# Linear attention and an ELU feed-forward layer on one core: the two halves of a quad of heads placed in neighbouring loop slots

## Chip, cores and metric

The kernel runs on one NeuronCore of a Trainium2 chip. The time is the device time of one execution in microseconds (us). The profile comes from one further execution of the same program; TensorE is called PE, VectorE DVE, ScalarE ACT, GpSimd POOL and SyncE SP, as in the profile.

## What is computed

Eight batches of eight heads go through a feature-map attention without softmax over the sequence; its output, heads side by side, is the input of a two-layer network with an ELU between.

```python
# q, k, v: (8, 8, 576, 64); w_phi: (64, 128)
def phi(x):
    proj = x @ w_phi
    proj = proj - max(abs(proj), axis=-1)
    return concatenate([exp(proj), exp(-proj)], axis=-1)
q_p, k_p = phi(q), phi(k)
kv, z = k_p^T @ v, sum(k_p, over the sequence)       # per head
x = (q_p @ kv) / (q_p @ z + 1e-6)
# x as (4608, 512); w_in: (512, 2048); w_out: (2048, 512)
h = x @ w_in
out = where(h > 0, h, exp(min(h, 0)) - 1) @ w_out
```

## The kernel before

**Quads.** A quad is four heads of one batch; there are 16 (`NQ`). Of the 576 positions of a head 512 are its main part, and 64 its tail; the tails of four heads of a quad share one tile. Each quad runs through a list of steps (`attention_steps`, L155):

- `transposes` (L159): PE transposes k and q of the quad, DVE copies them to SBUF (`kT`, `qT`).
- `k_head` five times, four heads and the tails (L212): PE projects (`pk`), DVE takes the maxima of absolute values (`m_k`, L203), ACT writes the two exponentials (`EK`, `EKt`, L216).
- `k_scale` (L221): ACT makes the scale factors `em` from `m_k`, and POOL multiplies v with them (`vs` four times, L230; `vst` twice for the tails, L241).
- `q_head` five times (L218): the maxima of q (`m_q`). `q_features` (L249) and `q_features_tail` (L263): PE computes the transposed features `pq`, ACT writes their exponentials (`Eq`, eight; `Eqt`, two) and `w`.
- `kv` twice (L284): PE sums k features times scaled v (`pkv`, L289 and L300), ACT casts it (`kv`, L308).
- `out_head` four times and `out_tail` (L310, L340): PE forms `pn`, DVE combines two of them into `tot` (L332, L338) or `tott`. `divide` (L365): DVE makes `den` and `rec`, POOL multiplies (`x` four times, L377; `xt`, L383). `x_out` (L390): PE transposes x, DVE copies it to `xT`, the input of the feed-forward part.

**Feed-forward (called MoE in the code).** A chunk is the 512 main rows of one batch; a ninth chunk holds all tails. `mm1` (L433) makes one of 16 slices of the hidden layer: four matmuls of 512 columns into `ph`, exponential on ACT (`e_sb`, L446), minus one on POOL (`u_sb`, L448), minimum and maximum on DVE (`gT`, L451). `mm2` (L455), four per chunk, is 16 matmuls of 512 columns into `po`, a copy on ACT (`o_sb`, L467) and a store by SP.

**Order.** The main loop (L494) issues the steps of quad after quad, each from the first step to the last, and between them the units (`mm1`, `mm2`) of the chunk of the batch before: half of the list beside the first quad of a batch, the rest beside the second. What is left runs after the loop. The compiler's scheduler then sets the order on every engine from the dependencies; each engine takes its instructions strictly in that order. All PSUM tiles of the attention share four buffers (`apsum`), those of `ph` and `po` another four (`mpsum`).

**Loads.** k, q, the tails and the weights are loaded by DMAs that POOL issues, v by DMAs that SP issues. Every eighth DMA of POOL shares a semaphore lane with the one eight earlier and waits for its completion before it is issued. `load_tails` (L100) is called for the first four quads (twelve DMAs) and, after `w_in` and `w_out`, for the other twelve quads (twelve DMAs); all of them stand on POOL ahead of the first `vs`.

Of the kernel before, what the change touches and what calls it, by code (L numbers as in the profile page):

```python
# [12 lines left out]
ACT = mybir.ActivationFunctionType  # L13
# [8 lines left out]
def kernel(  # L22
# [53 lines left out]
    w_in_sb = consts.tile([P, N_CT, DFF], BF16)  # L76
    w_in_r = moe_w_in.rearrange("(ct p) j -> p ct j", p=P)
# [21 lines left out]

    def load_tails(g0, g1):  # L100
        for src, dst, eng in (
            (k, k_tails, nc.gpsimd),
            (q, q_tails, nc.gpsimd),
            (v, v_tails, nc.gpsimd),
        ):
            flat = src.rearrange("b (g h) s d -> (b g) h s d", g=2)
            for s in range(2):
                for c in range(2):
                    eng.dma_start(
                        out=dst[s * TAIL:(s + 1) * TAIL, g0:g1, c, 0:D],  # L110
                        in_=flat[g0:g1, 2 * s + c, MAIN:S, :].rearrange(
                            "g j d -> j g d"
                        ),
                    )

# [39 lines left out]
    def attention_steps(i):  # L155
# [92 lines left out]

        def q_features(par, s):  # L249
            pq = apsum.tile([P, 4 * P], FP32, name="pq", tag="ap")  # L250
            nc.tensor.matmul(  # L251
                pq,
                w_phi_both[:, par, :],
                st["qT"][:, 4 * s:4 * s + 4, :].rearrange("p a b -> p (a b)"),
                start=True,
                stop=True,
            )
            for sg in range(2):
                nc.scalar.activation(  # L259
                    st["Eq"][:, par, s, sg, :], pq, ACT.Exp, scale=1.0 - 2.0 * sg  # L260
                )
# [22 lines left out]
        def kv(c):  # L284
# [12 lines left out]
            for s in range(2):  # L297
                for sg in range(2):
                    for t in range(NT):
                        nc.tensor.matmul(  # L300
                            pkv[:, s, sg, :],
                            st["EK"][:, 2 * s + c, sg, t * F:(t + 1) * F],
                            st["vs"][:, 2 * s + c, sg, t, :],
                            start=False,
                            stop=(t == NT - 1),
                            skip_group_check=True,
                        )
            nc.scalar.copy(st["kv"][:, c], pkv)  # L308

        def out_head(hh):  # L310
            s, c = divmod(hh, 2)
            if hh == 0:
# [5 lines left out]
            for sg in range(2):  # L318
                pt = apsum.tile([P, NT, D1], FP32, name=f"pn{sg}", tag="ap")
                for t in range(NT):  # L320
                    tp, par = divmod(t, 2)
                    o = (2 * c + tp) * P
                    nc.tensor.matmul(  # L323
                        pt[:, t, :],
                        st["Eq"][:, par, s, sg, o:o + P],
                        st["kv"][:, c, s, sg, :],
                        start=True,
                        stop=True,
                    )
                pn.append(pt)  # L330
# [34 lines left out]
        def divide():  # L365
# [9 lines left out]
            for hh in range(4):  # L375
                s, c = divmod(hh, 2)
                nc.gpsimd.tensor_tensor(  # L377
# [40 lines left out]
        return (
            [transposes]
            + [each(k_head, hh) for hh in range(5)]  # L420
            + [k_scale]
            + [each(q_head, hh) for hh in range(5)]
            + [each(q_features, par, s) for s in range(2) for par in range(2)]
            + [q_features_tail]
            + [each(kv, c) for c in range(2)]
            + [each(out_head, hh) for hh in range(4)]
            + [out_tail, divide, x_out]
        )

# [48 lines left out]

    def moe_units(ch):
        return [lambda jt=jt: mm1(ch, jt) for jt in range(N_JT)] + [  # L480
            lambda tt=tt: mm2(ch, tt) for tt in range(CHUNK // P)
        ]


    load_quad(0)
    load_tails(0, 4)
    load_quad(1)
    load_w_in()
    load_quad(2)
    load_w_out()  # L490
    load_tails(4, NQ)

    pending = []
    for i in range(NQ):  # L494
# [47 lines left out]
```

## Time and profile before

| | |
|---|---|
| runs (median of 3; lowest, highest) | 574.58 us (571.85, 575.05) |
| the profiled execution: its time, its span | 574.21 us, 572.4 us |
| mean granted clock of PE (1 is 2.4 GHz) | 0.901 |
| busy: PE, DVE, ACT, POOL | 416.2, 292.0, 264.8, 263.3 us |

The span runs from the first to the last instruction; the time of the execution is 1.81 us longer. Busy time is what an engine executes; an engine that waits for a semaphore is idle. The chain of waits follows the last instruction back to what released each step. In the windows the columns after the length are the busy times of PE, of PE's weight loads, of DVE, ACT and POOL with counts, then the granted clock, the share of the DMA engines and GB/s.

### The profile page before, as it was taken

Reading aid. Unit: us, or ns where it says so; the run is one execution under the profiler, and the core shown is the slowest. Engines: PE = TensorE matmul, PEld = TensorE weight load, DVE = VectorE, ACT = ScalarE, POOL = GpSimd, SP = SyncE. Lnnn points to the kernel's source line nnn. Section 1 sums busy time; section 2 is a strip of 40 time slices with the busy share of each in tenths; the row PEclk is TensorE's granted clock in tenths of the full one; section 3 lists DMA queues with packets and bytes.
Section 4 is the critical chain, followed back from the end, with each engine's and each line's share of the span. In section 5 each row is a group of like instructions: output and inputs, shape, how many; then the busy total and the mean of one; then the engine's idle time right before and its main releaser. Section 6 shows DMA issues by size and latency. Waiting matters only on the chain.

```text
span 572.4 us, 8389 instructions
## 1 busy us (share of the span) xinstructions
PE 416.2 (73%) x3066; PEld 232.1 (41%) x3120; DVE 292.0 (51%) x647; ACT 264.8 (46%) x581; POOL 263.3 (46%) x392
## 2 busy tenths in 40 slices
PE   2302557768866786868787896778768867789996
PEld 1102334434443443434344444444435434444443
DVE  2300646484548435763576466836484538527070
ACT  1600244654374518371836265635655373725251
POOL 7637234654365426551556236633644265426060
PEclk9855767799989799999988998999799979899999
DMA  9999312122312215041403231323100100010103
GB/s 161 194 198 137 47 38 37 38 38 73 74 38 38 50 54 82 1 74 57 84 10 57 73 57 38 42 70 74 38 0 35 42 1 2 19 56 1 74 1 73
DMA packets 71496, 32.55 MB, mean 57 GB/s; under 512 B 47904, under 2 KB 66336, under 8 KB 71456
## 3 DMA queue, kind: packets, MB, share of 16 engines
q0 software_dynamic: 32416, 14.19, 21.7%
q1 hardware_dynamic: 39040, 17.83, 11.8%
q8 instruction: 24, 0.39, 0.3%
q14 instruction: 16, 0.13, 0.1%
HBM read 36.77 MB, written 9.44 MB: 81 GB/s over the span
## 4 chain that ended last, share of the span: by engine, by line
PE 31%; POOL 26%; issue 16%; DVE 11%; ACT 9%; DMA 6%; POOLq 0%; ACTq 0%; DVEq 0%
POOL vs L230 11%; PE po L459 11%; PE ph L438 10%; POOL x L377 6%; ACT EK L216 6%; DVE gT L451 4%; POOL vst L241 3%; DMA w_out_sb<-in_moe_w_out_dram 3%; PE tr L167 3%; POOL u_sb L448 3%; DVE tot L332 2%; DVE tot L338 2%; PE pkv L300 2%; PE pk L196 2%; DMA w_in_sb<-in_moe_w_in_dram 2%
## 5 line engine op out<-in xcount | busy, mean ns | idle before, releaser
L438 PE MATMUL ph<-xT,w_in_sb 128*128 128x512 bf16 x482 | 136.1, 394 | 18.0 <-DVE gT L451 16.1
L448 POOL TENSOR_SCALAR u_sb<-e_sb 128x512 bf16<-128x512 f32 x144 | 88.1, 619 | 116.9 <-ACT e_sb L446 105.7
L451 DVE SCALAR_TENSOR_TENSOR gT<-u_sb,ph 128x512 bf16<-128x512 bf16 x144 | 95.7, 681 | 86.5 <-POOL u_sb L448 85.7
L459 PE MATMUL po<-w_out_sb,gT 128*128 128x512 bf16 x554 | 138.9, 389 | 0.8
L446 ACT ACTIVATE e_sb<-ph 128x512 f32<-128x512 f32 x144 | 89.6, 636 | 102.6 <-PE ph L438 79.1
L438 PEld LDWEIGHTS <-w_in_sb 128*128 128x128 bf16 x576 | 55.6, 101 | 68.2 <-issue 31.0
L230 POOL TENSOR_TENSOR vs<-v_main,em 128x520 bf16<-128x520 f32 x64 | 65.7, 1056 | 36.3 <-ACT em L224 36.3
L377 POOL TENSOR_TENSOR x<-tot,rec 128x256 bf16<-128x256 f32 x64 | 37.2, 614 | 92.1 <-DVE rec L374 91.0
L459 PEld LDWEIGHTS <-gT 128*128 128x128 bf16 x576 | 55.4, 100 | 57.9 <-issue 4.2
L216 ACT ACTIVATE EK<-pk 128x512 bf16<-128x512 f32 x128 | 64.6, 633 | 24.3 <-DVE m_k L203 24.3
L467 ACT COPY o_sb<-po 128x512 f32<-128x512 f32 x36 | 21.1, 586 | 114.4 <-PE po L459 114.4
L332 DVE TENSOR_TENSOR tot<-pn,w 128x260 f32<-128x260 f32 x64 | 24.9, 424 | 93.1 <-PE pn L323 92.8
L259 ACT ACTIVATE Eq<-pq 128x512 bf16<-128x512 f32 x128 | 67.6, 712 | 4.7 <-PE pq L251 4.7
L289 PE MATMUL pkv<-vst,EKt 128*128 128x130 bf16 x64 | 11.2, 271 | 72.8 <-POOL vst L241 52.7
L203 DVE TENSOR_REDUCE m_q<-pk 128x4 f32<-128x512 f32 (+1 forms) x80 | 48.4, 634 | 10.0 <-PE pk L196 9.0
L203 DVE TENSOR_REDUCE m_k<-pk 128x4 f32<-128x512 f32 (+1 forms) x80 | 46.4, 630 | 2.8 <-PE pk L196 2.5
L289 PEld LDWEIGHTS <-EKt 128*128 128x128 bf16 x64 | 6.7, 108 | 80.1 <-issue 69.6
L308 ACT CAST kv<-pkv 128x260 bf16<-128x260 f32 x32 | 12.0, 376 | 57.1 <-PE pkv L300 57.1
L196 PE MATMUL pk<-w_phi_both,qT 128*128 128x256 bf16 x144 | 28.1, 301 | 13.0 <-ACT EK L216 11.3
L394 PE MATMUL tr<-ident,x 128*128 128x128 bf16 x128 | 13.5, 232 | 24.9 <-POOL x L377 24.9
L401 DVE COPY xT<-tr 128x1024 bf16<-128x1024 bf16 x16 | 11.1, 692 | 39.2 <-PE tr L394 39.2
L196 PE MATMUL pk<-w_phi_both,kT 128*128 128x256 bf16 x144 | 25.0, 287 | 7.4 <-ACT EK L216 6.5
(61 smaller groups left out, 473.0 us busy)
## 6 DMA issues: line engine op xcount, KB each, us to landing
v_main<-in_v_dram SPq DMA_DIRECT2D x64, 128.0 KB, 2.6
out_dram<-o_sb SPq DMA_DIRECT2D x32, 256.0 KB, 2.3
k_main<-in_k_dram POOLq DMA_DIRECT2D x16, 256.0 KB, 4.4
q_main<-in_q_dram POOLq DMA_DIRECT2D x16, 256.0 KB, 4.9
w_in_sb<-in_moe_w_in_dram POOLq DMA_DIRECT2D x4, 512.0 KB, 9.6
w_out_sb<-in_moe_w_out_dram POOLq DMA_DIRECT2D x4, 512.0 KB, 17.3
out_dram<-o_sb SPq DMA_DIRECT2D x8, 128.0 KB, 2.3
k_tails<-in_k_dram POOLq DMA_DIRECT2D x4, 96.0 KB, 13.8
```

The costliest lines, as they stand in the source:

```text
L196: nc.tensor.matmul(pk[:, 2 * j:2 * j + 2, :].rearrange("p a b -> p (a b)"), xT[:, 2 * hh + j, :], w_phi_rhs, start=True, stop=True,)
L203: nc.vector.tensor_reduce(m[:, 4 * hh:4 * hh + 2 * n], pk[:, 0:2 * n, :], axis=AX.X, op=ALU.max, apply_absolute_value=True,)
L216: nc.scalar.activation(dst, pk, ACT.Exp, scale=1.0 - 2.0 * sg)
L230: nc.gpsimd.tensor_tensor(vs[:, hh], vb[:, hh:hh + 1].to_broadcast((P, 2, NT, D1)), em[:, :, 4 * hh:4 * hh + 4, None].to_broadcast((P, 2, ...
L259: nc.scalar.activation(st["Eq"][:, par, s, sg, :], pq, ACT.Exp, scale=1.0 - 2.0 * sg)
L332: nc.vector.tensor_tensor(tot, pn[1], st["w"][:, 4 * hh:4 * hh + 4, None].to_broadcast((P, NT, D1)), op=ALU.mult,)
L377: nc.gpsimd.tensor_tensor(st["x"][:, s, :, c, :], st["tot"][:, hh, :, 0:D], rec[:, 4 * hh:4 * hh + 4, None].to_broadcast((P, NT, D)), op=A ...
L438: nc.tensor.matmul(ph, w_in_sb[:, ct, jt * P:(jt + 1) * P], xTs[ch][:, ct, :], start=(ct == 0), stop=(ct == N_CT - 1),)
L446: nc.scalar.activation(e_sb, ph, ACT.Exp)
L448: nc.gpsimd.tensor_scalar(u_sb, e_sb, -1.0, 1.0, op0=ALU.add, op1=ALU.mult)
L451: nc.vector.scalar_tensor_tensor(gTs[ch][:, jt, :], u_sb, 0.0, ph, op0=ALU.min, op1=ALU.max)
L459: nc.tensor.matmul(po, gT[:, jt, tt * P:(tt + 1) * P], w_out_sb[:, jt, :], start=(jt == 0), stop=(jt == N_JT - 1),)
```

## The change

The loop now has 17 slots (n = 0 to 16). Slot n issues the first half of quad n (`k_head`, `k_scale`, `q_head`, `q_features`) beside the second half of quad n-1 (`kv`, `out_head`, `out_tail`, `divide`, `x_out`), alternating step by step, and at its end the transposes of quad n+1. The units of a chunk are listed in another way: after every fourth `mm1` of a chunk follows one `mm2` of the chunk before; the last chunk's `mm2` come at the end. The units of the chunk of batch b stand in slots 2b+3 and 2b+4, where they stood beside quads 2b+2 and 2b+3, and each chunk's `mm2` a whole chunk later, so more is left after the loop: 320 matmuls of 512 columns against 256.

The heads of a quad are paired in another way (first and second head instead of first and third in one group), which needs the rows of `w_in` in another order: eight DMAs of 64 partitions instead of four of 128. The tails are loaded by six DMAs per batch, 48 in all against 24. `w_out` is loaded in slot 1 instead of before the loop.

```diff
-            nc.gpsimd.dma_start(out=w_in_sb[:, ct, :], in_=w_in_r[:, ct, :])
+            for c in range(2):
+                nc.gpsimd.dma_start(
+                    out=w_in_sb[c * D:(c + 1) * D, ct, :],
+                    in_=w_in_r[ct // 2, c, ct % 2],
+                )
...
-    def load_tails(g0, g1):
...
+    def load_tails(b):
+        for src, dst in ((k, k_tails), (q, q_tails), (v, v_tails)):
+            heads = src[b].rearrange("(gc s) j d -> s j gc d", s=2)
             for s in range(2):
...
+                nc.gpsimd.dma_start(
+                    out=dst[s * TAIL:(s + 1) * TAIL, 2 * b:2 * b + 2, :, 0:D].rearrange(
+                        "p g c d -> p (g c) d"
+                    ),
+                    in_=heads[s, MAIN:S],
+                )
...
+    def slot_steps(n):
+        new = attention_steps(n) if n < NQ else None
+        old = quads.get(n - 1)
...
+        k = new["k"] if new else [None] * 5
+        qs = new["q"] if new else [None] * 5
+        if old:
+            steps += [old["kv"][0], k[0], old["kv"][1], k[1]]
+            for hh in range(3):
+                steps += [old["out"][hh], k[2 + hh]]
+            steps += [old["out"][3], new and new["scale"][0], old["out"][4]]
+        else:
+            steps += k + new["scale"]
+        steps += qs
+        if old:
+            steps += old["x"]
+        if new:
+            steps += new["qf"]
+            quads[n] = new
+        if n + 1 < NQ:
+            steps.append(lambda: transpose_next(n + 1))
+        return [f for f in steps if f]
...
+    def mixed_units(ch):
+
+        units = []
+        for jt in range(N_JT):
+            units.append(lambda jt=jt: mm1(ch, jt))
+            if ch > 0 and jt % 4 == 3:
+                units.append(lambda tt=jt // 4: mm2(ch - 1, tt))
+        return units
 
     load_quad(0)
-    load_tails(0, 4)
+    load_tails(0)
     load_quad(1)
     load_w_in()
     load_quad(2)
-    load_w_out()
-    load_tails(4, NQ)
-
+
+    transpose_next(0)
     pending = []
-    for i in range(NQ):
...
+    for n in range(NQ + 1):
+        steps = slot_steps(n)
+        share = len(pending) // 2 if n % 2 == 1 else len(pending)
         done = 0
...
+        if n == 1:
+            load_w_out()
+        if n + 3 < NQ:
+            load_quad(n + 3)
+        if n % 2 == 0 and n // 2 + 1 < B:
+            load_tails(n // 2 + 1)
+        if n > 0 and n % 2 == 0:
+            pending.extend(mixed_units(n // 2 - 1))
+    for unit in pending + mixed_units(B):
         unit()
+    for tt in range(CHUNK // P):
+        mm2(B, tt)
```

What the scheduler made of it stands below at three places; a count "x8" means that the instruction follows itself.

POOL at the start, from the load of `w_in` to the first `vs`. Before:

```order
L83 DMA w_in_sb<-in_moe_w_in_dram 128x2048 x4
L137 DMA k_main<-in_k_dram 128x4x256
L137 DMA q_main<-in_q_dram 128x4x256
L87 DMA w_out_sb<-in_moe_w_out_dram 128x4x512 x4
L109 DMA k_tails<-in_k_dram 64x12x64 x4
L109 DMA q_tails<-in_q_dram 64x12x64 x4
L109 DMA v_tails<-in_v_dram 64x12x64 x4
L230 TENSOR_TENSOR vs<-v_main_98,em 128x520 x4
```

Of the change, on to the first `x`:

```order
L84 DMA w_in_sb<-in_moe_w_in_dram 64x2048 x8
L136 DMA k_main<-in_k_dram 128x4x256
L136 DMA q_main<-in_q_dram 128x4x256
L229 TENSOR_TENSOR vs<-v_main_98,em 128x520 x4
L240 TENSOR_TENSOR vst_104<-v_tails,em 64x4x65 x2
L136 DMA k_main<-in_k_dram 128x4x256
L136 DMA q_main<-in_q_dram 128x4x256
L108 DMA k_tails<-in_k_dram 64x4x64 x2
L108 DMA q_tails<-in_q_dram 64x4x64 x2
L108 DMA v_tails<-in_v_dram 64x4x64 x2
L91 DMA w_out_sb<-in_moe_w_out_dram 128x4x512 x3
L229 TENSOR_TENSOR vs<-v_main_100,em 128x520 x4
```

The `vs` of quad 0 moved ahead of `w_out` and of all tails but those of batch 0; eleven DMAs now stand between it and the `vs` of quad 1. The tail loads of the later batches do not follow the batches: behind the first `xt` the scheduler put 23 DMAs in a row (k and q of two quads and 19 of tails) ahead of the `vs` of quad 2, and all the others before the `vs` of quad 3.

POOL in the middle of the program, from one `vs` to the next. Before:

```order
L230 TENSOR_TENSOR vs<-v_main_100,em 128x520 x4
L241 TENSOR_TENSOR vst_104<-v_tails,em 64x4x65 x2
L448 TENSOR_SCALAR u_sb<-e_sb 128x512 x10
L377 TENSOR_TENSOR x<-tot,rec 128x4x64 x4
L383 TENSOR_TENSOR xt<-tott,rec 128x128
L448 TENSOR_SCALAR u_sb<-e_sb 128x512 x2
L137 DMA k_main<-in_k_dram 128x4x256
L137 DMA q_main<-in_q_dram 128x4x256
L448 TENSOR_SCALAR u_sb<-e_sb 128x512
L230 TENSOR_TENSOR vs<-v_main_102,em 128x520 x4
```

Of the change:

```order
L229 TENSOR_TENSOR vs<-v_main_100,em 128x520 x4
L240 TENSOR_TENSOR vst_106<-v_tails,em 64x4x65 x2
L448 TENSOR_SCALAR u_sb<-e_sb 128x512
L376 TENSOR_TENSOR x<-tot,rec 128x4x64 x4
L382 TENSOR_TENSOR xt<-tott,rec 128x128
L448 TENSOR_SCALAR u_sb<-e_sb 128x512 x2
L136 DMA k_main<-in_k_dram 128x4x256
L136 DMA q_main<-in_q_dram 128x4x256
L448 TENSOR_SCALAR u_sb<-e_sb 128x512 x5
L229 TENSOR_TENSOR vs<-v_main_102,em 128x520 x4
```

Before, a `vs` and the `x` behind it belong to the same quad; now that `x` belongs to the quad before, and stands right behind the `vs` of the next one. Every quad has eight `u_sb` beside it; before it was thirteen or three by turns.

ACT in the middle of the program, from one `em` to the next `EK`. Before:

```order
L224 ACTIVATE em<-m_k 128x18 x2
L446 ACTIVATE e_sb<-ph 128x512
L259 ACTIVATE Eq<-pq 128x512 x8
L274 ACTIVATE Eqt<-pq 128x256 x2
L281 ACTIVATE w<-m_q 128x18
L308 CAST kv<-pkv 128x260 x2
L467 COPY o_sb<-po 128x512 x4
L446 ACTIVATE e_sb<-ph 128x512
L216 ACTIVATE EK<-pk 128x512 x8
```

Of the change, on to the next `em`:

```order
L258 ACTIVATE Eq<-pq 128x512 x8
L446 ACTIVATE e_sb<-ph 128x512
L273 ACTIVATE Eqt<-pq 128x256 x2
L467 COPY o_sb<-po 128x512
L307 CAST kv<-pkv 128x260 x2
L215 ACTIVATE EK<-pk 128x512 x2
L446 ACTIVATE e_sb<-ph 128x512
L215 ACTIVATE EK<-pk 128x512 x2
L446 ACTIVATE e_sb<-ph 128x512 x2
L215 ACTIVATE EK<-pk 128x512 x2
L215 ACTIVATE EKt<-pk 128x256 x2
L223 ACTIVATE em<-m_k 128x18 x2
```

The casts of `kv` belong to quad n-1 and stand behind the `Eq` of the same quad, as before; behind them now come the `EK` of quad n, no longer in one run of eight but with `e_sb` between them.

## Rows read from the trace of the kernel before

**Rows 1.** The page, section 1: busy us (share of the span) xinstructions.

```profile
PE 416.2 (73%) x3066; PEld 232.1 (41%) x3120; DVE 292.0 (51%) x647; ACT 264.8 (46%) x581; POOL 263.3 (46%) x392
```

**Rows 2.** Windows of the start, one batch in the middle, and the end; columns as above.

```profile
25.00:52.00 27.00, 0.00 (x0) 0.00 (x0) 0.00 (x0) 0.00 (x0) 14.28 (x18) 0.50 1.84 175
310.07:369.22 59.15, 46.95 (x374) 26.59 (x380) 35.16 (x79) 31.32 (x71) 28.72 (x42) 0.96 0.27 54
540.37:568.00 27.63, 27.47 (x125) 12.32 (x126) 10.92 (x16) 11.89 (x20) 9.88 (x16) 1.00 0.15 39
568.00:572.40 4.40, 0.01 (x1) 0.00 (x0) 0.00 (x0) 0.59 (x1) 0.00 (x0) 0.88 0.25 60
```

**Rows 3.** The chain that ended last, POOL's vs: start, us, what.

```profile
310.07 4.10 POOL vs L230 x4
...
340.98 4.07 POOL vs L230 x4
...
490.62 4.10 POOL vs L230 x4
```

**Rows 4.** Timeline of the start: start, us, engine, what, count [idle before <-releaser].

```profile
4.42 2.47 POOL L109 DMA_DIRECT2D k_tails<-in_k_dram  x4
...
18.91 0.34 ACT L224 ACTIVATE em<-m_k 128x18 f32<-128x18 f32 x2
...
22.62 0.75 POOL L87 DMA_DIRECT2D w_out_sb<-in_moe_w_out_dram  x1 [1.55 <-DMA w_in_sb<-in_moe_w_in_dram]
...
32.73 0.75 POOL L109 DMA_DIRECT2D k_tails<-in_k_dram  x1 [0.65 <-DMA q_main<-in_q_dram]
...
47.44 4.11 POOL L230 TENSOR_TENSOR vs<-v_main,em 128x520 bf16<-128x520 f32 x4
51.51 1.32 POOL L241 TENSOR_TENSOR vst<-v_tails,em 64x260 bf16<-64x260 bf16 x2
...
52.88 0.38 PE L289 MATMUL pkv<-vst,EKt 128*128 128x130 bf16 x2 [31.32 <-POOL vst L241]
...
54.17 0.38 ACT L308 CAST kv<-pkv 128x260 bf16<-128x260 f32 x1 [29.45 <-PE pkv L300]
...
60.70 2.32 POOL L377 TENSOR_TENSOR x<-tot,rec 128x256 bf16<-128x256 f32 x4 [6.35 <-DVE rec L374]
...
62.99 0.39 POOL L383 TENSOR_TENSOR xt<-tott,rec 128x128 bf16<-128x128 f32 x1
```

**Rows 5.** Timeline of one quad in the middle.

```profile
309.04 0.76 ACT L216 ACTIVATE EKt<-pk 128x256 bf16<-128x256 f32 x2
309.57 0.42 ACT L224 ACTIVATE em<-m_k 128x18 f32<-128x18 f32 x2
...
311.50 4.03 ACT L259 ACTIVATE Eq<-pq 128x512 bf16<-128x512 f32 x8 [1.03 <-PE pq L251]
...
315.34 0.74 ACT L274 ACTIVATE Eqt<-pq 128x256 bf16<-128x256 f32 x2
...
315.61 0.68 PE L300 MATMUL pkv<-vs,EK 128*128 128x65 bf16 x16
...
318.57 0.77 DVE L332 TENSOR_TENSOR tot<-pn,w 128x260 f32<-128x260 f32 x2 [1.70 <-PE pn L323]
```

**Rows 6.** Groups of instructions by form: busy us, mean ns | idle before.

```profile
L451 DVE SCALAR_TENSOR_TENSOR gT<-u_sb,ph 128x512 bf16<-128x512 bf16 x144 | 95.7, 681 | 86.5 <-POOL u_sb L448 85.7
L446 ACT ACTIVATE e_sb<-ph 128x512 f32<-128x512 f32 x144 | 89.6, 636 | 102.6 <-PE ph L438 79.1 <-PE pk L196 20.5 <-PE pn L323 2.3
L448 POOL TENSOR_SCALAR u_sb<-e_sb 128x512 bf16<-128x512 f32 x144 | 88.1, 619 | 116.9 <-ACT e_sb L446 105.7 <-DVE tot L338 6.9 <-DVE tot L332 2.3
```

**Rows 7.** PE's timeline behind an idle time in the middle.

```profile
346.38 0.38 PE L289 MATMUL pkv<-vst,EKt 128*128 128x130 bf16 x2 [3.27 <-ACT e_sb L446]
346.55 1.08 PE L300 MATMUL pkv<-vs,EK 128*128 128x65 bf16 x16
```

**Rows 8.** The window on these matmuls; columns as in rows 2.

```profile
346.50:348.00 1.50, 1.32 (x19) 1.13 (x18) 0.93 (x2) 0.83 (x4) 1.50 (x3) 0.50 0.36 82
```

More of the change, by code (lines that the diff above doesn't have):

```diff
@@ L259, in q_features @@
                 nc.scalar.activation(
-                    st["Eq"][:, par, s, sg, :], pq, ACT.Exp, scale=1.0 - 2.0 * sg
+                    st["Eq"][:, par, c, sg, :], pq, ACT.Exp, scale=1.0 - 2.0 * sg
                 )
@@ L301, in kv @@
                             pkv[:, s, sg, :],
-                            st["EK"][:, 2 * s + c, sg, t * F:(t + 1) * F],
-                            st["vs"][:, 2 * s + c, sg, t, :],
+                            st["EK"][:, 2 * c + s, sg, t * F:(t + 1) * F],
+                            st["vs"][:, 2 * c + s, sg, t, :],
                             start=False,
@@ L310, in out_head @@
         def out_head(hh):
-            s, c = divmod(hh, 2)
+            c, s = divmod(hh, 2)
             if hh == 0:
@@ L321, in out_head @@
                     tp, par = divmod(t, 2)
-                    o = (2 * c + tp) * P
+                    o = (2 * s + tp) * P
                     nc.tensor.matmul(
                         pt[:, t, :],
-                        st["Eq"][:, par, s, sg, o:o + P],
+                        st["Eq"][:, par, c, sg, o:o + P],
                         st["kv"][:, c, s, sg, :],
@@ L375, in divide @@
             for hh in range(4):
-                s, c = divmod(hh, 2)
+                c, s = divmod(hh, 2)
                 nc.gpsimd.tensor_tensor(
@@ L416, in each @@
             return lambda: f(*a)
[L418 to L428, printed above, removed]
+        return {
+            "tr": [transposes],
+            "k": [each(k_head, hh) for hh in range(5)],
+            "scale": [k_scale],
+            "q": [each(q_head, hh) for hh in range(5)],
+            "qf": [each(q_features, par, c) for c in range(2) for par in range(2)]
+            + [q_features_tail],
+            "kv": [each(kv, c) for c in range(2)],
+            "out": [each(out_head, hh) for hh in range(4)]
+            + [lambda: (out_tail(), divide())],
+            "x": [x_out],
+        }
     gTs = {}
@@ L477, in mm2, with transpose_next, attention_steps @@
                 )
[L479 to L482, printed above, removed]
+    def slot_steps(n):
+        new = attention_steps(n) if n < NQ else None
+        old = quads.get(n - 1)
+        nxt = []
+        steps = []
+        k = new["k"] if new else [None] * 5
[16 more added lines that the diff above has]
+        return [f for f in steps if f]
+    quads = {}
+    ready = {}
+    def transpose_next(n):
+        ready[n] = build_steps(n)
+        ready[n]["tr"][0]()
+    build_steps = attention_steps
+    def attention_steps(n):
+        return ready.pop(n)
+    def mixed_units(ch):
[5 more added lines that the diff above has]
+        return units
     load_quad(0)
-    load_tails(0, 4)
+    load_tails(0)
     load_quad(1)
@@ L489 @@
     load_quad(2)
-    load_w_out()
-    load_tails(4, NQ)
+    transpose_next(0)
     pending = []
-    for i in range(NQ):
-        b, qd = divmod(i, 2)
-        steps = attention_steps(i)
-        share = len(pending) if qd == 1 else len(pending) // 2
+    for n in range(NQ + 1):
+        steps = slot_steps(n)
+        share = len(pending) // 2 if n % 2 == 1 else len(pending)
         done = 0
-        for n, step in enumerate(steps):
+        for j, step in enumerate(steps):
             step()
-            upto = share * (n + 1) // len(steps)
+            upto = share * (j + 1) // len(steps)
             while done < upto:
```

25 lines of the change are left out of this document (3 added, 22 removed).

## The prediction

> **What bounds the kernel now.** I read the engine totals first: PE is busy 73% of the span, no other engine above 51% [rows 1]. None is full, so the time is made of waits, and the question is where. The windows by stage tell that [rows 2]. In 25 to 52 us PE executes nothing at all. In the middle a batch (two quads and one chunk) takes 59.15 us, in which PE is busy 46.95, DVE 35.16, ACT 31.32 and POOL 28.72 us. In the last windows 128 matmuls of 512 columns take 27.63 us with PE busy 27.47: there PE is the bound, at 0.216 us per matmul and a clock of 1.00. The chain of waits names what the middle waits for: a `vs` on POOL leads every quad, at 310.07, 340.98 and, six quads after the first of these, at 490.62 [rows 3], so a quad takes 180.55 / 6 = 30.1 us. The timeline of the start names the first wait: POOL issues `w_out` and the later tails before the first `vs`, waiting for landings, until 47.44; PE has waited 31.32 us for `vst` when it goes on at 52.88 [rows 4].
>
> **The change, 1: the start.** The first `vs` now stands behind k and q of quad 2, not behind `w_out`. The q load waits for the second half-load of `w_in`, which is the first quarter of `w_in` together with the one before it; that quarter had landed at 22.62 [rows 4]. Six tail DMAs fewer stand ahead, for which I take off 2 us, and one issue (0.75) follows: `vs` at 21.3. Its `em` was ready at 19.3 [rows 4]. `vs` and `vst` take 4.11 and 1.32, so the first `kv` matmul moves from 52.88 to about 26.8, the cast behind it, at 54.17, to 28. Four more `w_in` issues are covered by the same waits for landings; without the cover they would be some 2 us.
>
> **2: slots 1 to 4.** I count a slot from the first `kv` cast to the next one. In slot 1 POOL issues eleven DMAs before the `vs` of quad 1, the third `w_out` only when the first new tail has landed. Quad 2's q had landed at 32.73 with twelve tails ahead [rows 4], now some 30.7; behind it k and q of quad 3 and the tail, 1.3 us each: `vs` at about 35.5, done 40.9, one more issue, `x` and `xt` (2.32 and 0.39 [rows 4]) done 44.4. Then comes what I call the return: transposes, first `pq`, eight `Eq` in 4.03, two `Eqt` in 0.74 [rows 5], cast: 6 us without MoE work. Slot 2 begins at 51. There POOL first issues 23 DMAs, four at 0.75 and 19 at 2.47 / 4 = 0.62 [rows 4], 14.8 us: `vs` of quad 2 runs from 59.2 to 64.6, a tail DMA and `x` to 68, the return to 75. Issued in slots 4, 6 and on, as the text of the loop reads, these loads would cost the same issues later; here they hold one `vs` by 2 us at most, as its `em` is ready at 57. Slots 3 and 4 have eight `mm1` and no `mm2` each: I take 25 us, between this slot and the full one below. Slot 5 begins at 125.
>
> **3: a full slot.** Eight `mm1` and two `mm2` beside one quad. The time is not a sum of an engine's work but a ring through the fixed orders of ACT, DVE and POOL, which comes back to the `kv` cast:
> - From the first cast to the last `m_k`: the second `kv` group and its cast end 1.0 later. ACT then does two `EK`, 1.0 (eight `Eq` in 4.03 give 0.5 for each that follows another [rows 5]), and an `e_sb` of 0.64; `u_sb` takes 0.62 [rows 6]; the `gT` for it stands on DVE ahead of the third `m_k`. From there DVE has in a row: three `gT` and two `m_k` of 0.6 (0.68 for a `gT` alone, less the overlap [rows 6]), four `tot` operations of 0.4 [rows 5], a short `m_k` of 0.4, with one `gT` more already under way: 5.0. Sum 8.2.
> - `EKt` and `em`: 0.76 and 0.42 [rows 5] with the hand-over, 1.3.
> - POOL: `vs`, `vst` 5.4, one `u_sb` 0.6, and only then `x`, `xt` 2.7 [rows 4]: 8.7. `rec`, which `x` needs too, is ready some 2 us before POOL comes to it, so POOL's order is what ends last.
> - The return, with an `e_sb` and an `o_sb` in ACT's order and the `mm2` matmuls on PE that wait for the PSUM buffers of `Eq`: 0.7 + 4.0 + 0.5 + 0.75 + 1.1 + 0.4 = 7.5, with hand-overs 7.7.
>
> Together 26 us against 30.1: the pipelining takes the long `vs` wait out of the quad's own chain, but `x` of the quad before now queues behind it. PE's own work is less: 64 matmuls at 0.216 are 13.8; the attention of a quad is at most (46.95 - 27.6) / 2 = 9.7 [rows 2], and by its 15,568 columns at the rate of the last window 6.6. So PE has 20.4 to 23.5 us of work in 26 and is not the bound. Slots 5 to 15: 11 x 26 = 286. Slot 16 begins at 411.
>
> **4: the end.** Behind the last first cast PE has half a chunk's list (64 matmuls) and the 320 left after the loop: 384 x 0.216 = 82.9, and some 2.7 for the last quad's second half. The last copy and store stay at 4.40 [rows 2]. Sum: 411 + 82.9 + 2.7 + 4.4 = 501, and 1.8 us around the span: 503. The profiled execution took 574.21, the median is 574.58: the sum stands on nearly the same time. I take **502 us**.
>
> The new order of `w_in`'s rows and of the heads costs nothing in the steps: the instructions keep their forms and counts. The other price the trace does not show is that of more semaphore hand-overs in the ring: zero if all hide, 0.1 for each of twenty if none does: 24 to 28 us per slot, 480 to 524 in all.
>
> **The rivals.**
> (a) *PE becomes the bound.* If DVE and ACT run ahead of the orders I followed, a slot lasts as long as PE's work, 20.4 to 23.5, say 22. Then 11 x 4 us come off: 458. For it: PE has the most work in every window of the middle. Against it: `x` cannot start before `vs` ends on POOL. The Trainium skill, Perfetto Trace Analysis, Optimization Strategy, says that interleaving stages with different limiting engines may improve the time; in the trace the middle and the end do have different limits [rows 2], but the ring is a limit of no engine's total.
> (b) *The wait before `x` cools PE.* In each slot PE runs out of matmuls some 2 to 3 us before `x` is ready. After an idle time of 3.27 us, 16 `pkv` matmuls ran with a granted clock of 0.50, which is 1.2 GHz, and took 1.08 us instead of the 0.68 in the quad shown [rows 5, 7, 8]. In the return PE has about 5 us of work at full clock; if it mostly runs at half, the slot grows by 3 us: 502 + 33 = 535. Against it: in the middle the clock was 0.96 on the mean, with such waits in it [rows 2].
> (c) *The lower clock holds through the slot.* Then the kernel gets slower: with a share f of PE's 22 us at half clock a slot takes 22 (1 + f). The old time is reached when eleven slots take 72 us more, that is 32.5 us, f = 0.48; at f = 0.6, with 35 us, it is 601. For it: the units, once in runs, are cut into ones and twos between small matmuls of the attention. The Trainium skill, Perfetto Trace Analysis, Matmul Optimizations, says that the matmul engine scales its power with use and that matmuls should come in back-to-back batches; by that rule this rival's side gains. Against it: the window of one batch has the same small matmuls and 0.96.
> (d) *The change does not do what it says.* For the tail loads that is so (they are not spread over the batches), and counted above. For the halves the orders on ACT and POOL show the new interleaving; I give it no chance of its own.
>
> **How the numbers follow.** Forecast (24 to 28 us a slot) 0.62; (a) 0.16; (b) 0.18; (c) 0.04. Range 457 to 536: it holds the forecast's case, most of (b) and the upper half of (a). A difference of 0.5% is about what a measurement of this kernel can tell from none (its three runs spread by 0.56%). Only (c) ends on the slow side: faster 0.96, same 0.01, slower 0.03.
>
> **What would show it.** Right: `vs` starts at about 21 us and every 26 us in the middle; `x` follows `vst` and one `u_sb` on POOL without a gap; the window of a batch lasts 52 us; after the last `x` some 73 us of dense PE. Wrong: `x` waiting for `rec` rather than for POOL (my DVE part is too short), a granted clock near 0.5 behind each `x` wait (b, c), PE without idle time in the middle (a), or a first `vs` well behind 21 us.

## The result and the profile after

The changed kernel takes **508.8 us** (median of 4 runs, 507.1 to 509.8) against 573.2 for the kernel before on the same chip: ratio **0.888, 95% interval 0.883 to 0.893**. That is 64 us or 11.2% faster. Predicted were 502 us, range 457 to 536. The profiled execution took 507.1 us, with a span of 505.3. The page, section 1 and the clock by slices, which answer to [rows 1]:

```profile
span 505.3 us, 8410 instructions
PE 409.6 (81%) x3070; PEld 223.1 (44%) x3120; DVE 306.1 (61%) x647; ACT 268.3 (53%) x581; POOL 278.5 (55%) x420
PEclk9965959797989899989999999999998999899999
```

PE has nearly the same matmuls and the same busy time as before, in a span 67 us shorter. Windows of the changed kernel, which answer to [rows 2] (start, one batch in the middle, the end and what follows it; columns: start:end, length, then busy us and count of PE, PEld, DVE, ACT, POOL, the granted clock, DMA share, GB/s):

```profile
27.00:52.00 25.00, 14.44 (x113) 8.73 (x112) 11.42 (x28) 9.91 (x23) 19.42 (x29) 0.59 1.30 189
229.00:280.00 51.00, 45.47 (x367) 25.16 (x372) 36.38 (x78) 31.43 (x70) 28.79 (x42) 0.97 0.33 63
411.00:430.00 19.00, 16.53 (x125) 8.49 (x126) 11.18 (x25) 6.50 (x13) 7.63 (x13) 0.99 0.07 28
430.00:500.00 70.00, 69.69 (x313) 31.47 (x318) 21.92 (x32) 25.99 (x44) 19.77 (x32) 0.98 0.14 45
500.00:505.30 5.30, 0.54 (x3) 0.04 (x1) 0.00 (x0) 0.59 (x1) 0.00 (x0) 0.94 0.24 56
```

The start, where PE did nothing, now holds 14.44 us of its work. A batch (two slots, 24.9 and 26.5) takes 51.4 us instead of 59.15, with nearly the same busy times. The kernel leaves 64 matmuls more for the end; at the 0.216 us each of the dense stretch [rows 2] they are 13.8 us (an estimate) by which the end is longer.

Where the time went is read off three points: the first `kv` cast, the same cast of the last quad, and the end. Before, the first cast stood at 54.17 [rows 4], and the last quad's was this row of ACT's timeline:

```profile
496.88 0.38 ACT L308 CAST kv<-pkv 128x260 bf16<-128x260 f32 x1 [0.20 <-PE pkv L300]
```

After, the two rows are:

```profile
27.69 0.38 ACT L307 CAST kv<-pkv 128x260 bf16<-128x260 f32 x1 [4.83 <-PE pkv L299]
...
411.14 0.51 ACT L307 CAST kv<-pkv 128x260 bf16<-128x260 f32 x1
```

So the start gave 54.17 - 27.69 = 26.5 us. The fifteen quads between took 442.7 us before and 383.4 now (29.5 and 25.6 each): 59.3 us. The end took 75.5 us before and 94.2 now: 18.7 us given back. Together 67.1 us, the difference of the two spans (572.4 and 505.3).

### The profile page after: what moved, and what is told of

Same layout as the page of the kernel before. It is cut to its first block, busy times and chain, and to the rows that moved or that the text cites. A ratio compares the mean times of both kernels' runs of the same rounds, so it can differ in the third digit from the quotient of the medians.

```text
span 505.3 us, 8410 instructions
## 1 busy us (share of the span) xinstructions
PE 409.6 (81%) x3070; PEld 223.1 (44%) x3120; DVE 306.1 (61%) x647; ACT 268.3 (53%) x581; POOL 278.5 (55%) x420
## 4 chain that ended last, share of the span: by engine, by line
PE 52%; POOL 20%; DVE 13%; DMA 6%; issue 4%; ACT 4%; POOLq 0%; ACTq 0%
PE po L459 22%; PE ph L438 13%; POOL x L376 7%; DMA q_main<-in_q_dram 5%; POOL vs L229 4%; DVE m_q L202 4%; PE pq L250 4%; PE pn L322 3%; PE pkv L299 2%; POOL vst L240 2%; PE pk L195 2%; ACT EK L215 2%; POOL u_sb L448 2%; PE tr L166 2%; DVE den L367 2%
## 5 line engine op out<-in xcount | busy, mean ns | idle before, releaser
L459 PE MATMUL po<-w_out_sb,gT 128*128 128x512 bf16 x559 | 148.1, 389 | 1.8 <-DVE gT L451 1.4
L438 PE MATMUL ph<-xT,w_in_sb 128*128 128x512 bf16 x480 | 131.0, 390 | 4.6 <-DVE gT L451 3.4
L446 ACT ACTIVATE e_sb<-ph 128x512 f32<-128x512 f32 x144 | 87.3, 611 | 48.8 <-PE ph L438 46.8
L215 ACT ACTIVATE EK<-pk 128x512 bf16<-128x512 f32 x128 | 69.4, 612 | 13.1 <-DVE m_k L202 13.0
L202 DVE TENSOR_REDUCE m_k<-pk 128x4 f32<-128x512 f32 (+1 forms) x80 | 50.4, 632 | 25.9 <-PE pk L195 25.6
L322 PEld LDWEIGHTS <-Eq 128*128 128x128 bf16 x512 | 28.9, 98 | 24.9 <-issue 17.0
L393 PEld LDWEIGHTS <-x 128*128 128x128 bf16 x128 | 8.4, 108 | 68.8 <-POOL x L376 68.8
L322 PE MATMUL pn<-kv,Eq 128*128 128x65 bf16 x512 | 34.0, 194 | 3.8 <-ACT EK L215 2.6
L136 POOL DMA_DIRECT2D k_main<-in_k_dram x16 | 12.8, 802 | 35.9 <-PE tr L166 25.3
L195 PE MATMUL pk<-w_phi_both,kT 128*128 128x256 bf16 x144 | 29.6, 284 | 3.3 <-ACT EK L215 1.0
L171 DVE COPY kT<-tr 128x1024 bf16<-128x1024 bf16 x16 | 11.1, 692 | 34.1 <-PE tr L166 34.1
```

The source lines that it names most:

```text
L195: nc.tensor.matmul(pk[:, 2 * j:2 * j + 2, :].rearrange("p a b -> p (a b)"), xT[:, 2 * hh + j, :], w_phi_rhs, start=True, stop=True,)
L202: nc.vector.tensor_reduce(m[:, 4 * hh:4 * hh + 2 * n], pk[:, 0:2 * n, :], axis=AX.X, op=ALU.max, apply_absolute_value=True,)
L215: nc.scalar.activation(dst, pk, ACT.Exp, scale=1.0 - 2.0 * sg)
L322: nc.tensor.matmul(pt[:, t, :], st["Eq"][:, par, c, sg, o:o + P], st["kv"][:, c, s, sg, :], start=True, stop=True,)
L438: nc.tensor.matmul(ph, w_in_sb[:, ct, jt * P:(jt + 1) * P], xTs[ch][:, ct, :], start=(ct == 0), stop=(ct == N_CT - 1),)
L446: nc.scalar.activation(e_sb, ph, ACT.Exp)
```

## The experiments

Eleven kernels were run, each against the kernel before on the same chip, in several runs of each. The ratios can therefore be compared across the groups. "Against the change" below is the ratio less 0.8879, times 573.2 us; the intervals of a ratio are 0.003 to 0.007 either way, so a difference below some 4 us is not told from none.

| run | median us | ratio (95%) | against the change, us |
|---|---|---|---|
| the change | 508.8 | 0.888 (0.883 to 0.893) | |
| e1_no_pipeline | 558.0 | 0.976 (0.972 to 0.980) | +50 |
| e2_unmixed | 515.4 | 0.902 (0.899 to 0.905) | +8 |
| e3_w_out_early | 520.4 | 0.911 (0.906 to 0.916) | +13 |
| e4_pool_before_x | 517.3 | 0.905 (0.901 to 0.909) | +10 |
| e5_pool_after_x | 508.1 | 0.888 (0.882 to 0.894) | 0 |
| e6_x_before_vs | 513.0 | 0.897 (0.892 to 0.903) | +5 |
| e7_q_heads_late | 532.9 | 0.932 (0.926 to 0.937) | +25 |
| e8_both | 490.9 | 0.859 (0.852 to 0.866) | -17 |
| e9_busy_wait | 523.5 | 0.918 (0.914 to 0.921) | +17 |
| e10_tails_held | 500.7 | 0.878 (0.875 to 0.882) | -6 |
| e11_both_held | 485.2 | 0.851 (0.847 to 0.855) | -21 |

### The parts of the change, undone one by one

**The pipelining** (the loop over quads runs all steps of a quad in sequence again; the new loads and the mixed units stay):

```diff
-    for n in range(NQ + 1):
-        steps = slot_steps(n)
...
+    for n in range(NQ):
+        b, qd = divmod(n, 2)
+        st = build_steps(n)
+        steps = [
+            f
+            for part in ("tr", "k", "scale", "q", "qf", "kv", "out", "x")
+            for f in st[part]
+        ]
```

> The steps of a quad stand one after another again; the mixed list of units, the new loads and the pairing of heads stay. Theory (the ring through ACT, DVE and POOL; the start and the pipelining are two separate gains): the start keeps its gain of 26 us, a quad takes its own chain of about 30 us again, so 545 to 555 us. Rival (the mixed units and the new loads bring the gain, the two halves side by side little): at most 520 us.

Measured 558.0 us, a ratio of 0.976: 3 us beyond what was expected, and far from the rival. By the same three points (casts at 28.03 and 467.99, span 555.7) the start keeps its 26 us and a quad takes 29.3 us, as before (29.5), so the theory held there; what it left out is the end, 87.7 us against 75.5. So the early start and the mixing alone leave 2.4% of the 11.2%; some 50 of the 64 us hang on this edit. It is not the pipelining alone: the transposes are no longer made a slot ahead, and `w_out` is loaded in slot 0. The first `vs` starts as early as in the change, at 21.30, but the second only at 55.82 (38.44 in the change). Its `em` had been ready since 46.8; POOL's load issues, three of them waiting 1.9 to 2.2 us each for `w_out`, held it 9 us. Behind this first slot a slot takes 29.0 us on the mean of fourteen, against 25.5 in the change: 48 us, the price of the pipelining together with the early transposes.

**The mixing** (all `mm2` of a chunk behind its `mm1` again):

```diff
-            if ch > 0 and jt % 4 == 3:
-                units.append(lambda tt=jt // 4: mm2(ch - 1, tt))
+        for tt in range(CHUNK // P):
+            units.append(lambda tt=tt: mm2(ch, tt))
```

> The two halves stay side by side; the units of a chunk are listed as before, 16 mm1 and then 4 mm2, so that a slot has ten mm1, or six mm1 and four mm2, by turns. Theory: a slot follows the ring, in which an e_sb more or less moves POOL's and DVE's part by some 0.6 us each, up and down by turns, and 64 matmuls fewer are left after the loop: 500 to 514 us. Rival (the mixing is what lets PE run on, without it the mm1 slots are bound by DVE): 530 us or more.

Measured 515.4 us: the rival falls, and the theory's range is missed by 1 us on the slow side. The mixing is worth 8 us on balance. From the casts (27.97 and 433.78) and the span (513.6), a slot without it takes 27.1 us on the mean instead of 25.6, which is 22 us over fifteen slots, and the end, with 64 matmuls fewer, is 14 us shorter (79.8 against 94.2). That longer and shorter slots would balance was wrong.

**The late `w_out`** (loaded ahead of the loop again):

```diff
     load_quad(2)
+    load_w_out()
...
-        if n == 1:
-            load_w_out()
```

> w_out is loaded before the loop again, all else as in the change. Theory (the twelve tail loads behind w_out, not w_out, held the first vs): the four issues wait for the fifth and sixth half of w_in, so the first vs starts at 24 instead of 21 us, and the second one has fewer issues ahead of it: 506 to 514 us. Rival (w_out itself held the first vs): the first vs at 35 us or later, 520 us or more.

Measured 520.4 us: the rival's time, but not its reason. The first `vs` stands at 26.5. What is later still is the second one, as POOL's timeline shows:

```profile
26.51 4.09 POOL L229 TENSOR_TENSOR vs<-v_main,em 128x520 bf16<-128x520 f32 x4
...
37.74 0.62 POOL L108 DMA_DIRECT2D q_tails<-in_q_dram  x1 [2.52 <-DMA w_out_sb<-in_moe_w_out_dram]
41.07 0.61 POOL L108 DMA_DIRECT2D v_tails<-in_v_dram  x1 [2.71 <-DMA w_out_sb<-in_moe_w_out_dram]
44.46 0.61 POOL L108 DMA_DIRECT2D v_tails<-in_v_dram  x1 [2.78 <-DMA w_out_sb<-in_moe_w_out_dram]
...
52.44 4.10 POOL L229 TENSOR_TENSOR vs<-v_main,em 128x520 bf16<-128x520 f32 x4
```

Three tail loads of 0.6 us each wait 2.5 to 2.8 us for parts of `w_out` to land, and the second `vs` queues behind them, at 52.44 instead of 38.44. Of these 14 us, 5.5 come from the first `vs`. Between the two, sixteen DMAs stand on POOL where the change has eleven (eight of them, for later quads, are issued there only behind `xt`), and their waits add up to 10.1 us where the change has 4.6. So moving `w_out` pays less by its own four issues than by what waits behind it: both theories had the price at the wrong `vs`. The run also tells what freed the first `vs`: with `w_out` still ahead of it, it starts 21 us earlier than in the kernel before, because the tail loads of the later quads no longer stand between them.

### Is a slot a ring?

The forecast rested on the claim that a slot lasts as long as a chain through the fixed orders of ACT, DVE and POOL, and that only work in that chain counts. Two kernels add the same work to POOL, one of the four ops of `x` computed once more (about 0.6 us) in each slot. In the first it stands ahead of the rest of `x`, in the second right behind `xt`, where nothing waits for it:

```diff
-            for hh in range(4):
+            for hh in (0, 0, 1, 2, 3):
```

```diff
+            x_again = work.tile([P, NT, D], BF16, name="x_again", bufs=1)
+            nc.gpsimd.tensor_tensor(
+                x_again,
+                st["tot"][:, 0, :, 0:D],
+                rec[:, 0:4, None].to_broadcast((P, NT, D)),
+                op=ALU.mult,
+            )
```

> POOL does the first x of each quad twice, 0.6 us more of POOL ahead of the rest of x; the output is the same. Theory (x on POOL is part of the ring): each of 16 slots 0.6 us longer, 516 to 520 us, and a batch in the middle 52.5 us instead of 51.4. Rival (PE's work sets the slot): within 2 us of the change, since POOL is busy 55% of the span.

> The first half of x is computed once more on POOL right behind the last op of the quad's tail there (xt), where no other engine waits for it: the same added POOL work as in the run that put it before x. Ring theory (a slot is the chain first cast, last m_k, em, vs, vst, x, cast, and only what stands in it counts): within 2 us of the changed kernel, 507 to 511 us. Rival (POOL's total work in a slot sets the time, wherever it stands): about 516 to 520, as with the op before x.

Measured: +10 us in the chain, 0 us beside it. The chain decides, and POOL's total does not. Not all of the 10 us is the 0.6 us itself. From cast to cast a slot of e4 takes about 25.4 or 26.8 us, where the change has 24.9 or 26.5, so 0.5 and 0.3 us more; and seven of its eleven full slots are of the long kind, five in the change. What makes a slot long is shown two sections on.

### What the ring is made of

The other edits move work within the slot. `e6_x_before_vs` holds `vs` of quad n on POOL until `xt` of quad n-1 is issued:

```diff
-            steps += [old["out"][3], new and new["scale"][0], old["out"][4]]
+            steps += [old["out"][3], old["out"][4], new and new["scale"][0]]
...
-            nc.gpsimd.tensor_tensor(
+            behind["xt"] = nc.gpsimd.tensor_tensor(
                 st["xt"],
...
             for hh in range(4):
-                nc.gpsimd.tensor_tensor(
-                    vs[:, hh],
+                with tc.issue_after(behind["xt"].ins) if behind else ExitStack():
+                    nc.gpsimd.tensor_tensor(
+                        vs[:, hh],
```

> On POOL the values of quad n are scaled (vs) behind the tail of quad n-1 (vst, x, xt) instead of before it. Ring theory: x no longer stands behind vs, 4.11 us, but starts when rec is there (246.37 against 247.77 in one slot), some 1 to 1.4 us earlier in each of 15 slots, and vs ends about 5 us later than now but still before the state kv of its quad needs it: 493 to 502 us. Rival (the later vs holds up kv and with it the tail of its own quad): 509 to 525.

Measured 513.0 us, 5 us slower: a miss for the ring theory as I had filled it in, and the rival's time without its reason. The first four slots end 4 us earlier than in the change (slot 5 begins at 126.06, not 129.82), so the eleven full slots lose more than the 5 us, about 11. `x` did come 1.2 us earlier (4.8 us behind the moment at which `em` lets POOL go on, instead of 6.0), but it was not `kv` that the later `vs` held up. The timelines of POOL, of DVE and of PE in e6:

```profile
248.38 4.10 POOL L231 TENSOR_TENSOR vs<-v_main,em 128x520 bf16<-128x520 f32 x4
252.45 1.20 POOL L450 TENSOR_SCALAR u_sb<-e_sb 128x512 bf16<-128x512 f32 x2
```

```profile
253.10 1.29 DVE L453 SCALAR_TENSOR_TENSOR gT<-u_sb,ph 128x512 bf16<-128x512 bf16 x2 [3.72 <-POOL u_sb L450]
254.31 0.68 DVE L172 COPY kT<-tr 128x1024 bf16<-128x1024 bf16 x1
```

```profile
255.04 0.22 PE L175 MATMUL trt<-ident,k_tails 128*128 128x128 bf16 x1 [2.38 <-DVE kT L172]
...
255.15 3.61 PE L461 MATMUL po<-w_out_sb,gT 128*128 128x512 bf16 x9
```

Two `u_sb` now stand behind `vs`; DVE waits 3.72 us for them with a `gT`, and the copy of the next quad's transposes, `kT`, waits in DVE's order behind that `gT`. In the changed kernel it starts 6.0 us after `x` (7.6 in a long slot), here 8.6. PE then waits 2.38 us for this copy, a wait that the changed kernel does not have, and in two slots of three the granted clock falls behind it (0.58 from 255.0 to 258.5; 1.00 from 310 to 313, in the third): the nine `po` that follow take 3.61 us, and 2.10 us in the third slot and in the changed kernel. Such a slot lasts 27.9 us and the third 26.2, against 24.9 in the changed kernel where the clock stays. The new wait was on an engine I had not followed.

`e7_q_heads_late` moves the q units of the new quad behind the `x` step of the old one:

```diff
-        steps += qs
         if old:
             steps += old["x"]
+        steps += qs
```

> The q units of quad n are recorded behind the x step of quad n-1 instead of before it, so that VectorE and ScalarE reach rec earlier; the order on POOL (vs, vst, u_sb, x) is left as it is. Ring theory: POOL's order holds x (x waits for rec 3 times only, 3.0 us in all), so nothing is won: 505 to 511 us. Rival (rec, through VectorE's q work, is what x waits for): 485 to 500.

Measured 532.9 us, 25 us slower, which neither theory had. PE's timeline in e7:

```profile
264.30 1.18 PE L393 MATMUL tr<-ident,x 128*128 128x128 bf16 x8 [3.86 <-POOL x L376]
265.27 0.31 PE L405 MATMUL trt<-ident,xt 128*128 128x128 bf16 x1
265.37 1.06 PE L195 MATMUL pk<-w_phi_both,qT 128*128 128x256 bf16 x4
```

The first half stands as said: POOL's order still holds `x` (6.04 us behind the start of `vs`, as in the changed kernel). But the maxima of q, which ran beside the wait for `x`, now run behind it: from the start of `x` to the first `Eq` it is 7.3 us instead of 3.2, and to the next cast 12.3 instead of 9.7 or 11.3. Work taken off the cover of a wait went into the ring. PE's wait before x also grew, from 2.23 to 3.86 us, and behind it the granted clock was 0.50 (1.2 GHz) in the window from 264.20 to 266.00.

`e8_both` makes both edits.

> Both edits together: vs behind the tail of the quad before on POOL, and the q units behind x. Ring theory: rec comes some 2 us earlier and POOL is free for x then, so the ring falls from 25.6 to about 22.5 us a slot, where the TensorE work of a slot (about 22.7 us) is as long: 465 to 485 us. Rival (TensorE without the q units beside the wait for x cools, its clock falls, and the slot stays at 25 us or more): 500 to 525.

Measured 490.9 us, 17 us faster than the change, between the two theories. The chain shortens in one part and lengthens in another. POOL's timeline of e8:

```profile
259.69 1.31 POOL L242 TENSOR_TENSOR vst<-v_tails,em 64x260 bf16<-64x260 bf16 x2 [1.50 <-DVE gT L453]
262.59 0.62 POOL L450 TENSOR_SCALAR u_sb<-e_sb 128x512 bf16<-128x512 f32 x1 [1.59 <-issue]
263.17 2.33 POOL L378 TENSOR_TENSOR x<-tot,rec 128x256 bf16<-128x256 f32 x4
265.46 0.40 POOL L384 TENSOR_TENSOR xt<-tott,rec 128x128 bf16<-128x128 f32 x1
265.81 4.11 POOL L231 TENSOR_TENSOR vs<-v_main,em 128x520 bf16<-128x520 f32 x4
...
284.24 1.32 POOL L242 TENSOR_TENSOR vst<-v_tails,em 64x260 bf16<-64x260 bf16 x2 [1.49 <-DVE gT L453]
```

`x` starts 3.5 us behind the moment at which `em` lets POOL go on, instead of 6.0; the q work stands in the return, but `vs` runs beside it. A slot is 24.6 us (`vst` to `vst`), not the 22.5 that I had expected, because from `x` to the next such moment it now takes 21.1 us (18.9 in a short slot of the change). Before the transposes of x, PE waits 1.3 us, and the clock does not fall behind that wait (next section). Against a short slot of the change (24.9) the chain is only 0.3 us shorter; the larger part of the gain in the middle is that no slot is a long one.

### The clock behind the wait for x

The full slots of the change alternate: 24.9 and 26.5 us from cast to cast (257.45, 283.92, 308.82, 335.29 in ACT's timeline). Windows behind the wait for `x`, in a short slot and in a long one:

```profile
249.50:252.00 2.50, 2.19 (x15) 1.20 (x17) 0.93 (x2) 1.22 (x4) 2.12 (x5) 1.00 0.00 0
275.40:278.00 2.60, 2.55 (x9) 0.99 (x10) 2.01 (x4) 2.06 (x4) 1.12 (x2) 0.61 0.00 0
```

and PE's rows at the two places, with the same wait:

```profile
249.59 0.40 PE L393 MATMUL tr<-ident,x 128*128 128x128 bf16 x4 [2.23 <-POOL x L376]
...
274.48 0.40 PE L393 MATMUL tr<-ident,x 128*128 128x128 bf16 x4 [2.23 <-POOL x L376]
```

In the long slot the granted clock is 0.61 in this stretch, nine matmuls fill what fifteen did not fill in the other, and the return takes 8.6 instead of 7.0 us. In both slots PE executes the same instructions in the same order from this wait to the cast, so it is the clock and not other work that makes one longer. To keep PE busy in the wait, `e9_busy_wait` puts transposes of the identity in front of those of x:

```diff
+            for t in range(24):
+                nc.tensor.transpose(tr[:, t % 2, t // 2 % NT, :], ident, ident)
```

> TensorE gets 24 more transposes of the identity, about 1.5 us of work at some 0.06 us each, in front of the eight transposes of x, where it stood idle for 2.23 us; their results are written over. If the fall of the clock behind that wait (granted 0.61 to 0.72 in every second slot) is what makes every second slot 26.4 instead of 24.9 us: the clock stays at 1.0, all full slots take 24.9 us, and the time falls by some 9 us, to 498 to 502 us. Rival (slots alternate because the two quads of a batch carry different MoE work): 506 to 511 us.

Measured 523.5 us, 17 us slower; both theories miss. PE's timeline of e9, and the window behind it:

```profile
253.87 1.50 PE L392 MATMUL tr<-ident 128*128 128x128 bf16 x24
257.56 1.18 PE L395 MATMUL tr<-ident,x 128*128 128x128 bf16 x8 [2.19 <-POOL x L376]
```

```profile
258.50:260.00 1.50, 1.28 (x7) 0.68 (x6) 0.96 (x2) 0.69 (x2) 0.51 (x1) 0.50 0.00 0
```

The edit did not fill the wait: the instructions added to PE made the scheduler place MoE matmuls elsewhere (14 `po` in a row stand before `kv` now, nine in a short slot of the change), and 2.19 us of idle time stayed. The clock falls behind it in this slot and the next (0.50 from 285 to 287), and a slot is 27.6 us; the one that ends at 322.09, where the clock is 1.00 behind the same idle time, is 26.4 us. So this run doesn't tell what would happen without the wait. Its rival, that the two quads of a batch carry different MoE work, falls nevertheless: besides the equal order on PE, the long slots come two in three in e6 and almost always here, not one per batch. What the windows of four kernels show behind a wait is a granted clock of 0.50 behind 3.86 us (e7), 0.50 or 1.00 behind 2.2 us (e9), 0.61 or 1.00 behind 2.23 us (the change), and 1.00 behind 1.30 us in e8:

```profile
264.00:265.00 1.00, 0.01 (x1) 0.02 (x2) 0.00 (x0) 0.17 (x1) 1.00 (x3) 1.00 0.00 0
265.00:267.00 2.00, 1.77 (x16) 1.23 (x18) 1.01 (x3) 0.00 (x0) 2.00 (x4) 1.00 0.00 0
```

Why every second wait of the change costs clock, and the one between doesn't, is open.

### The tail loads, and the best version

The loads written "per batch" do not run per batch. Nothing they overwrite is in use, so the order on POOL has those of batches 2 to 4 ahead of the scaling of quad 2. `e10_tails_held` keeps them behind the `xt` of their slot:

```diff
-                nc.gpsimd.dma_start(
+                with tc.issue_after(behind["xt"].ins) if behind else ExitStack():
+                    nc.gpsimd.dma_start(
```

> The tail loads of the later batches are held behind the x step of their slot on POOL, so that the 14 DMAs for batches 2 to 4 no longer stand in front of the scaling (vs) of quad 2. Ring theory: that vs then starts when its em is there, at about 62.9 us instead of 64.86, so some 2 us are won and the rest of the DMA time was hidden: 504 to 508 us. Rival (the DMAs cost their full 9 us): 497 to 501 us.

Measured 500.7 us, in the rival's range; by the ratios, which take out the chip, it is 6 us below the change and between the two theories. In the change, and then in e10 (POOL's timeline):

```profile
64.23 0.67 POOL L108 DMA_DIRECT2D k_tails<-in_k_dram  x1
64.86 2.13 POOL L229 TENSOR_TENSOR vs<-v_main,em 128x520 bf16<-128x520 f32 x2
```

```profile
60.44 4.09 POOL L231 TENSOR_TENSOR vs<-v_main,em 128x520 bf16<-128x520 f32 x4 [6.75 <-ACT em L225]
```

With the loads gone, `vs` waits for `em` and comes 4.4 us earlier. I had put it at 62.9, with the 9.2 us of a full slot; this slot has no MoE units beside it, and 6.7 us pass from its first cast (53.77) to `vs`. The slot takes 20.7 us instead of 26.7.

`e11_both_held` is e8 with this edit.

> The two reorderings together (vs behind the tail of the quad before, q units behind x) and the tail loads held. There slot 2 took 29.8 us, from the kv cast at 53.54 to that at 83.30, because the x of quad 1 stood behind the later batches' tail loads on POOL until 70.25; a slot of 24.6 there saves about 5 us: 482 to 488 us. Rival (the first slots wait for the landings of the loads anyway): 489 to 492 us.

Measured **485.2 us, ratio 0.851 (0.847 to 0.855)**: as expected, and the fastest of all, 15% below the kernel before and some 21 us below the change. Its middle, in one window:

```profile
229.00:280.00 51.00, 45.58 (x378) 25.67 (x382) 36.11 (x83) 32.85 (x73) 32.41 (x49) 1.00 0.39 69
```

PE is still idle for a tenth of it, so the ring of 24.7 us on the mean, and not PE, should be the limit here too; no run tested it for this kernel.

## Why the prediction was right, point by point

Forecast and measurement by the steps of the sum:

| point | predicted, us | measured, us |
|---|---|---|
| first `vs` / first cast | 21.3 / 28 | 20.97 / 27.69 |
| second `vs` | 35.5 | 38.44 |
| slot 2 begins | 51 | 53.73 |
| `vs` of quad 2 | 59.2 | 64.86 |
| slot 3 / slot 5 begins | 75 / 125 | 80.39 / 129.82 |
| slot 16 begins | 411 | 411.14 |
| from there to the end of the span | 90 | 94.2 |

**1, the start**, holds to 0.3 us. Of the 26.5 us by which the first `vs` is earlier, e3 puts 5.5 on `w_out`. The other 21 are those of the later quads' tail loads, which with their waits kept POOL from 25.8 to 47.4 in the kernel before.

**2, slots 1 to 4**, were mis-sized by 5 us. In slot 1 the issues of `w_out` ahead of the second `vs` wait for the landings of the quad loads, as counted, but the landings came later and further apart: the last tail load, which waits for q of quad 2, was issued at 32.53, not 30.7, and from there it took 2.1 and 2.3 us to the next two waiting issues, not 1.3. Only the third `w_out` did not wait. POOL's timeline:

```profile
34.64 0.75 POOL L91 DMA_DIRECT2D w_out_sb<-in_moe_w_out_dram  x1 [1.50 <-DMA k_main<-in_k_dram]
36.89 1.49 POOL L91 DMA_DIRECT2D w_out_sb<-in_moe_w_out_dram  x2 [1.50 <-DMA q_main<-in_q_dram]
```

In slot 2 the 23 DMAs took 17.6 us, from 47.24 to 64.86, not 14.8: the issues themselves were as predicted, but four of them waited, 2.9 us in all. So "here they hold one `vs` by 2 us at most" fails: `em` was there at 60.3, and `vs` was held 4.5 us. e10 shows the price. That the text of the loop spreads these loads and the kernel doesn't was right.

**3, a full slot**, was 26 and is 25.57 on the mean of eleven. The timelines of ACT, of DVE and of POOL in one long slot of the changed kernel, one after the other:

```profile
257.45 0.38 ACT L307 CAST kv<-pkv 128x260 bf16<-128x260 f32 x1
...
265.67 0.66 ACT L215 ACTIVATE EKt<-pk 128x256 bf16<-128x256 f32 x2 [0.26 <-DVE m_k L202]
266.21 0.33 ACT L223 ACTIVATE em<-m_k 128x18 f32<-128x18 f32 x2
...
283.92 0.38 ACT L307 CAST kv<-pkv 128x260 bf16<-128x260 f32 x1
```

```profile
265.22 0.41 DVE L202 TENSOR_REDUCE m_k<-pk 128x2 f32<-128x256 f32 x1
...
271.26 0.25 DVE L373 RECIPROCAL rec<-den 128x18 f32<-128x18 f32 x1
```

```profile
266.62 4.11 POOL L229 TENSOR_TENSOR vs<-v_main,em 128x520 bf16<-128x520 f32 x4 [1.49 <-ACT em L223]
270.69 1.31 POOL L240 TENSOR_TENSOR vst<-v_tails,em 64x260 bf16<-64x260 bf16 x2
272.08 0.62 POOL L448 TENSOR_SCALAR u_sb<-e_sb 128x512 bf16<-128x512 f32 x1
272.67 2.33 POOL L376 TENSOR_TENSOR x<-tot,rec 128x256 bf16<-128x256 f32 x4
274.95 0.40 POOL L382 TENSOR_TENSOR xt<-tott,rec 128x128 bf16<-128x128 f32 x1
```

Part by part: first cast to the end of the last `m_k` 8.2 (8.2 predicted); `EKt` and `em` 1.0 (1.3); `vs` to `xt` 8.7 (8.7); the return 8.6 in this slot and 7.0 in the ones between (7.7). `rec` is ready 1.2 us before `x` starts, not 2, and POOL's order binds, as said. e4 and e5 show that this chain, not POOL's total, sets the slot. e6 to e8 show that the chain holds only for this order: with `vs` behind `x` it runs through DVE's `gT` and `kT`.

**4, the end**, was 4 us short. Of its 94.2 us PE is busy 86.8, for which 82.9 + 2.7 = 85.6 stood in the sum. It is idle for 2.5 us from 411 to 430, at the last wait for `x`, which the sum did not have, and for 4.8 behind 500, where it had 4.4.

The rivals. (a), PE as the bound, did not come: PE's wait for `x` stands in every slot. (b), the wait before `x` cools PE, came in a small form: in every second slot, and for 1.5 us instead of 3, some 8 us in all. It is why the slot is a mean of two lengths. (c) did not come: the clock of a batch is 0.97. The Trainium skill, Perfetto Trace Analysis, Matmul Optimizations, says that matmuls should execute back to back in batches. Read as a rule on the list of units it speaks for the unmixed one; here that list is 8 us slower (e2), with a granted clock of 0.94 and 0.97 in two batches of its middle against 0.97. (d) was right for the tail loads alone.

Since the errors of step 2 and 4 (+5 and +4 us) and of step 3 (-5 us) partly cancel, the sum was nearer than its terms: 505.3 against a predicted span of 501. That slot 16 begins at 411 as forecast is such luck.

## What to carry to other kernels

Where no engine is full and a software pipeline is to be judged, follow the chain through the in-order queues of all engines until it comes back to its first instruction: the slot is its length, work beside it was free here, and the same work inside it counted almost in full. When an instruction is moved on one queue, list what then stands behind it and which instruction of another engine waits for that; here a 4 us op moved behind `x` won 1.2 us and lost more through two `u_sb` of 0.6 us. When a wait on PE grows or moves, read the granted clock behind it too: in e8 that was worth more than the shorter chain. Loads without a hazard are placed by the scheduler, not by the line they are written on: read the order on the issuing engine before counting on a spread.

## What the runs showed of the hardware that was not expected

- The same idle time of 2.23 us on PE was followed by a granted clock of 0.61 in one slot and 1.00 in the next, regularly, at 1.5 us a slot, while 1.30 us (e8) was followed by 1.00. A wait of 2.38 us (e6) was followed by a fallen clock in two slots of three.
- DMA issues of 0.6 us on POOL waited 2.5 to 2.8 us each for the landing of earlier, larger loads (e3), three times with 8.0 us in all. With five DMAs more ahead of it, the second `vs` came 14 us later than in the change, while the first was 5.5 late.
